# Stored sums in two parts, output weights' pieces at rest for one group, and five half tiles of x in an attention-mix kernel

## The chip, the cores and the metric

The kernel runs on one core of one Trainium2 chip. The metric is the time of one execution on the device in microseconds, as the median of several runs. One execution of the kernel before was also recorded by the hardware profiler; all rows shown here come from that record. The engines are named as the profile names them: PE (TensorE, matmul), PEld (its weight load), DVE (VectorE), ACT (ScalarE), POOL (GpSimd) and SP (SyncE, which issues most transfers).

## The reference

Two attention blocks on the same input of 2048 rows and 1024 columns, 32 heads of 32, mixed by a gate. All in float32.

```python
def _A_ref(x, wqkv, wo):
    ...
    phi = lambda t: jnp.where(t > 0, t + 1, jnp.exp(t)) + 1e-6
    pq, pk = phi(q), phi(k)
    kv = jnp.einsum("bhsd,bhse->bhde", pk, v)
    z = jnp.einsum("bhsd->bhd", pk)
    num = jnp.einsum("bhqd,bhde->bhqe", pq, kv)
    den = jnp.einsum("bhqd,bhd->bhq", pq, z)[..., None] + 1e-6
    o = num / den
    return (lambda x, *d: x.transpose(*d))(o, 0, 2, 1, 3).reshape(B, S, D) @ wo

def _B_ref(x, wqkv, wo):
    ...
    scores = jnp.einsum("bhqd,bhkd->bhqk", q, k) * (Dh ** -0.5)
    p = _softmax(scores, axis=-1)
    o = jnp.einsum("bhqk,bhkd->bhqd", p, v)
    return (lambda x, *d: x.transpose(*d))(o, 0, 2, 1, 3).reshape(B, S, D) @ wo

x = A_x
g = _sigmoid((x * gate_w).sum(-1, keepdims=True))
a = _A_ref(x, A_wqkv, A_wo)
b = _B_ref(x, B_wqkv, B_wo)
return g * a + (1 - g) * b
```

## The kernel before

**Numbers in two parts.** A float32 operand is split into a high part, rounded to the matmul's format by a cast on ScalarE, and a low part, the difference, by a subtraction (`split`, lines 293 to 295: L294 is the cast, L295 the subtraction). A product is three matmuls, high by high, high by low and low by high (`three`, L153, L156, L158), each 128 x 128 by 128 x 512. Results collect in eight PSUM banks.

**Stages, in order of time.**

1. The first v pass (0 to some 50 us): values of block B for the first half of the rows (J = 0), one 128-row piece k of the weights at a time (`load_block`, `split_wv`, `split_x`, `v_pass`). Eight small matmuls on a tile of ones (L627) stand ahead of the first product.
2. The first set of groups, J = 0. Queries and keys of block B are computed for all heads with Strassen's scheme in Winograd's form: seven products instead of eight, on sums and differences of the inputs and the weights. A group (`quad`) makes seven products of twelve matmuls, each into its own bank, combines them on VectorE, and stores four sums. There are eight groups, numbered 0 to 7 here; `quads` runs 0 to 6 of them, and the eighth runs with `change()` beside it.
3. The second v pass (J = 1), begun near 205 us, and the second set of eight groups, near 257 to 410 us, the eighth with `leave()` beside it.
4. The last v pass, from about 410 us to some 523 us: the other 512 columns of v, over all sixteen 128-row units (the stream `linear`, kind "v"). From its middle on the heads' row maxima (`maxima`, L1240 and L1245) and the gate (`gate_step`) run beside it.
5. The heads (some 525 to 2660 us): 32 heads of block B, with scores, exponentials (L1385), sums on POOL (L1467), products with v (L1532), beside the rest of `linear`: block A's keys and values, queries and output.
6. The output of block B (`output`), with Strassen products again, to the end.

**Who orders the work.** Every engine runs its own instructions in the order in which the program writes them. In stages 1 to 3 that order is written out by hand. From stage 4 on a planner writes it: it keeps reckoned clocks for the engines (`T`), costs for each step, and times at which data are reckoned to be there (`xp_ready`, `w_ready`, `q_ready`), and takes the stream that can go on soonest.

**A group and its side work.** `next(side, None)` inside `quad` is one step of side work, seven in a group. The side streams that `quads` runs together are the next group's weights (`quad_weights`, lines 420 to 443, six steps), the late sums of x, transfers, and the pieces of block B's output weights (`parts`). A step of the first, second and third kind writes, for instance, `tensor_sub(w21, w11, w21)` (L432) and then a split. In `change()` and `leave()` the steps are splits.

A group combines and stores like this: the copy of product 0 (L467), the addition of product 1 (L469) and the first store; the additions L476, L477, L478 and the second store; L482, L483 and the third store; L486 and the fourth store. A store (`store`) casts the sum's high part on ScalarE, subtracts on VectorE and issues two transfers of 256 KB to DRAM on SP.

**The pieces of the output weights** (`wo_parts`). 28 pieces are made on POOL: a cast (L513), a subtraction (L514), two transfers (L516), and after three pieces of every seven one more subtraction (L524, L531, L537), with loads of raw weights on POOL's queue (L502). A piece is let go by a tiny copy on ScalarE (L511) that POOL's own tiny copy (L512) waits for. `PIECE_STEP` spaces them: `wait()` lets a turn pass per step until 3.4 turns are over, and each wait uses one turn without giving a step away. Of the 28 pieces, numbers 0 to 18 go out in the first set, one in group 0 and three in each of groups 1 to 6; numbers 19 to 27 go out in the second set: three in group 0, two in group 1, three in group 2, the last at the first step of group 3.

**x in half tiles.** In `linear` each unit of 128 rows needs x in four row pieces of 2 halves: half m = 2n + 0 or 1, with a high and a low part, each 256 KB. Before there are three half tiles, used in turn (`xh_t`): two are the halves of `big[4]`, the third is `xh`. Units 0 to 3 of the last v pass read x from tiles that are still there; the first three halves are asked for at unit 1, and when half m has been used, half m + 3 is asked for. The v weights' store, the heads' v loads (`load_v`), the gate's x loads and the raw weights of the next stage go through the same queue on SP.

**The rows.** For each head the row maxima are turned by a matmul, split (`mh`, `ml`) and written by four transfers into the last rows of the query tiles: `q_first` holds the first 512 columns, `q_rest` the others (`rows`, lines 1247 to 1270).

**The output.** Its first six products (X11 and T1 of three pairs of row tiles) run beside the heads; their banks are copied out on ScalarE (L1695). After the heads come the splits of the next operands (`prep`), the loads of block A's result (`load_ra`) and the other products; results are added on VectorE (L1704 and following).

## Time and profile before

| what | value |
|---|---|
| median of 3 runs | 2822.71 us (2821.43 to 2822.95) |
| the profiled execution: its own time | 2824.52 us |
| its span in the profile | 2822.7 us |
| TensorE's granted clock, mean | 0.998 |
| chain that ended last | TensorE 90%, DMA 2%, "issue" 1% |
| HBM read, written | 314.31 MB, 127.66 MB |
| matmuls | 15880 |

A row of a timeline gives the start in us, the duration in us, the engine, the line of the program, the operation, output and inputs by the program's names, their shapes, and in brackets how long the engine was idle ahead of it and what ended that. SPq and POOL rows of kind DMA are the issuing alone. A row of waits gives the waiting instruction, whom it waited for, the total in us, how often, and the longest. A row of stretches gives the stretch and its length, then busy time and number of instructions of PE, PEld, DVE, ACT and POOL, the granted clock of TensorE as a share of full speed, the mean busy share of the 16 DMA engines, and GB/s. Matmuls are pipelined and their ends are modelled, so that a matmul of 512 columns shows 0.39 us where the next one starts 0.23 us later.

### The profile page before, as it was taken

To read this page: it belongs to the slowest core of one execution; us is meant where nothing else is said; L and a number is where in the kernel's file an instruction comes from. 1 tells how busy PE (TensorE), PEld (TensorE's weight loads), DVE (VectorE), ACT (ScalarE), POOL (GpSimd) and SP (SyncE) were. 2 spreads that over 40 slices of the span, in tenths; PEclk is the share of its full clock that TensorE was granted. 3 is DMA by queue.
4 is the path that set the end of the run, shared out by engine and by line. 5 is a ranking of instruction groups with operands and counts; after the bars stand their busy time and mean duration, and the time that the engine had idled before them with its cause. 6 is when DMAs were issued, how large, how long until landed. Compare 5 with 4: busy or idle time off the path is not lost.

```text
span 2822.7 us, 47003 instructions
## 1 busy us (share of the span) xinstructions
PE 2801.9 (99%) x15880; PEld 2043.3 (72%) x15880; DVE 2330.5 (83%) x3745; ACT 1638.2 (58%) x3095; POOL 2104.1 (75%) x1150
## 2 busy tenths in 40 slices
PE   9999999999999999999999999999999999999999
PEld 8877887777767776677766777776676667666687
DVE  7887865888878888888888888888877888886688
ACT  5334332566666666666766666676666666666522
POOL 0651433699999999999899988989889988888000
PEclk9999999999999999999999999999999999999999
DMA  8997979533343434333433444456575555544774
GB/s 279 301 335 224 293 224 282 175 100 102 103 127 97 106 98 131 94 98 102 126 105 96 106 131 129 151 167 186 172 213 159 145 158 146 145 121 140 255 238 152
DMA packets 403340, 459.52 MB, mean 163 GB/s; under 512 B 106894, under 2 KB 234894, under 8 KB 401308
## 3 DMA queue, kind: packets, MB, share of 16 engines
q1 hardware_dynamic: 381084, 419.03, 47.5%
q0 software_dynamic: 22016, 37.50, 6.2%
q8 instruction: 126, 2.06, 0.3%
q14 instruction: 114, 0.93, 0.1%
HBM read 314.31 MB, written 127.66 MB: 157 GB/s over the span
## 4 chain that ended last, share of the span: by engine, by line
PE 90%; DMA 2%; issue 1%; DVE 0%; ACT 0%; SPq 0%; ACTq 0%; DVEq 0%
PE bank L1382 17%; PE bank L1240 16%; PE bank L1532 16%; PE bank L153 13%; PE bank L156 13%; PE bank L158 13%; PE bank L1304 1%; PE bank L1026 1%; PE bank L915 0%; DMA big<-ra 0%; DMA xh<-xs 0%; SPq L170 0%; PE bank L1296 0%; DMA qk<-mid 0%; DVE big L295 0%
## 5 line engine op out<-in xcount | busy, mean ns | idle before, releaser
L1467 POOL TENSOR_TENSOR big<-big,big 128x512 f32<-128x512 f32 (+2 forms) x694 | 1641.7, 2369 | 107.5 <-ACT big L1385 64.4
L1245 DVE TENSOR_REDUCE mx<-bank 128x1 f32<-128x512 f32 x2048 | 1313.5, 682 | 305.9 <-PE bank L1240 301.9
L1385 ACT ACTIVATE big<-bank 128x512 f32<-128x512 f32 x2048 | 1179.6, 602 | 433.7 <-PE bank L1382 368.4
L1382 PE MATMUL bank<-big,big 128*128 128x512 f32 x1888 | 742.4, 394 | 2.2 <-DMA big<-ml 2.2
L1240 PE MATMUL bank<-big,big 128*128 128x512 f32 x1888 | 739.8, 392 | 1.1 <-ACT big L1385 1.1
L153 PE MATMUL bank<-big,big 128*128 128x512 f32 x1576 | 618.1, 392 | 9.2 <-DVE mid L486 3.9
L158 PE MATMUL bank<-big,big 128*128 128x512 f32 x1572 | 614.9, 391 | 0.5 <-DMA big<-xs 0.2
L156 PE MATMUL bank<-big,big 128*128 128x512 f32 x1576 | 615.4, 390 | 0.0
L1532 PE MATMUL bank<-big,mid 128*32 128x512 f32 x4096 | 454.2, 593 | 0.0
L1382 PEld LDWEIGHTS bank<-big,big 128*128 128x128 f32 x1888 | 354.5, 188 | 127.3 <-issue 48.1
L1240 PEld LDWEIGHTS bank<-big,big 128*128 128x128 f32 x1888 | 355.0, 188 | 75.0 <-ACT big L1385 2.4
L153 PEld LDWEIGHTS bank<-big,big 128*128 128x128 f32 x1576 | 296.9, 188 | 77.6 <-ACT big L294 4.5
L158 PEld LDWEIGHTS bank<-big,big 128*128 128x128 f32 x1572 | 295.8, 188 | 65.9 <-DVE big L295 3.0
L156 PEld LDWEIGHTS bank<-big,big 128*128 128x128 f32 x1576 | 296.7, 188 | 61.3 <-DVE big L295 0.2
L1532 PEld LDWEIGHTS bank<-big,mid 128*32 128x32 f32 x4096 | 143.9, 110 | 264.1 <-issue 263.8
L1483 DVE TENSOR_TENSOR bank<-bank,big 128x512 f32<-128x512 f32 x364 | 251.5, 691 | 5.3 <-ACT big L1385 2.9
L295 DVE TENSOR_TENSOR big<-mid,big 128x512 fp32r<-128x512 f32 (+1 forms) x157 | 122.2, 795 | 44.6 <-ACT big L294 44.2
L294 ACT CAST big<-mid 128x512 fp32r<-128x512 f32 (+1 forms) x157 | 92.8, 618 | 113.1 <-DVE mid L1651 66.0
L1463 POOL TENSOR_TENSOR big<-big,big 128x1536 f32<-128x1536 f32 (+1 forms) x31 | 122.9, 3964 | 44.8 <-ACT big L1385 44.8
L153 PE MATMUL bank<-big,xh 128*128 128x512 f32 x376 | 147.1, 391 | 2.4 <-DMA xh<-xs 2.4
L158 PE MATMUL bank<-big,xh 128*128 128x512 f32 x376 | 146.9, 391 | 0.0
L156 PE MATMUL bank<-big,xh 128*128 128x512 f32 x376 | 146.8, 390 | 0.0
(163 smaller groups left out, 2123.0 us busy)
## 6 DMA issues: line engine op xcount, KB each, us to landing
big<-xs SPq DMA_DIRECT2D x288, 256.0 KB
big<-qk SPq DMA_DIRECT2D x690, 64.0 KB
xh<-xs SPq DMA_DIRECT2D x144, 256.0 KB
qk<-mid SPq DMA_DIRECT2D x128, 256.0 KB
big<-oA SPq DMA_DIRECT2D x84, 256.0 KB
xs<-big SPq DMA_DIRECT2D x64, 256.0 KB
oA<-mid SPq DMA_DIRECT2D x64, 256.0 KB
big<-big POOLq DMA_DIRECT2D x50, 256.0 KB, 5.4
```

The costliest lines, as they stand in the source:

```text
L153: yield nc.tensor.matmul(ps, sh, mh_, start=(kt == 0), stop=False)
L156: yield nc.tensor.matmul(ps, sh, ml_, start=False, stop=(late and last))
L158: yield nc.tensor.matmul(ps, sl, mh_, start=False, stop=last)
L295: eng.tensor_sub(lo, src, f32(hi))
L1240: nc.tensor.matmul(bank[b], q[:, t % TPC * P:(t % TPC + 1) * P], k[:, j * C:(j + 1) * C], start=True, stop=True)
L1245: nc.vector.tensor_reduce(m[:, t, j:j + 1], bank[b], AX.X, ALU.max)
L1382: nc.tensor.matmul(bank[b], k[:, t * P:(t + 1) * P], q_cols(h, j), start=True, stop=True)
L1385: nc.scalar.activation(pr_t[i][:, j * C:(j + 1) * C], bank[b], AF.Exp, scale=SCALE)
L1463: nc.gpsimd.tensor_add(lacc[:, :qp], pr(0)[:, :qp], pr(1)[:, :qp])
L1467: nc.gpsimd.tensor_add(lacc[:, sl], lacc[:, sl], pr(t)[:, sl])
L1483: nc.vector.tensor_add(lacc[:, qp:] if t == NT - 1 else l_b[:, :n], l_b[:, :n], src)
L1532: nc.tensor.matmul(av_b[j * DH:(j + 1) * DH, :], v[:, t, :], pr(t)[:, j * C:(j + 1) * C], start=(t == 0), stop=(t == NT - 1))
```

## The change

Six edits:

- `store` casts the sum's high part, then takes a step of side work, then subtracts and issues its two transfers. The four steps that followed the stores in `quad` go away, so that a group still has seven steps.
- `PIECE_REST = 2`: in the first set the stream `parts` is cut off after 42 steps, six groups instead of seven; it goes on in the second set. By the count of steps, pieces 0 to 15 then go out in the first set, and 16 to 27 in the second: three in group 0, three in group 1, two in group 2, three in group 3, the last in group 4. No piece falls away.
- The last v pass reads x from five half tiles, the two new ones being the halves of `big[5]`. Five halves are asked for at unit 1. `load_past(m)` asks for half m + 5; the three tiles of old serve again from half 32 on, and it is placed ahead of the storing of mixed weights and of `load_v`.
- In `load_block` the v weights of the first piece are loaded ahead of the first 128 columns of x.
- In `rows` the four transfers go in the order high and low for the first columns, then high and low for the others.
- In `output` the copy of the last T1 product out of its bank waits until the first two of the three following `prep` steps are written.

The assignments of 0 to `xp_ready` for the halves 0 to 2, which fall away, name halves that are never loaded.

```diff
@@ -1,6 +1,6 @@
 from collections import deque
 from contextlib import ExitStack
-from itertools import count
+from itertools import count, islice
 
 import concourse.bass as bass
 import concourse.tile as tile
@@ -39,7 +39,7 @@
 WARM = 8
 NE = 3
 AHEAD_X = 3
-PIECE_STEP = 3.4
+PIECE_STEP, PIECE_REST = 3.4, 2
 GATE_STEP, GATE_FROM = 2.3, 20.0
 LATE = 1.0
 MANUAL = {ET.PE, ET.DVE, ET.Activation, ET.SP, ET.Pool}
@@ -133,7 +133,7 @@
 
     k_stack = [big[1], big[3]]
     q_first, q_rest = [big[0][:, :C], big[2][:, :C], None], [big[0], big[2]]
-    xh_t = [big[4][:, :D], big[4][:, D:], None]
+    xh_t = [big[4][:, :D], big[4][:, D:], None, big[5][:, :D], big[5][:, D:]]
     w_t = big[16:20]
     PR, SPARE, LACC = (6, 7, 8, 9, 10, 11, 15, 5, 14), 12, (13, 20)
 
@@ -459,7 +459,9 @@
             return ps
 
         def store(i, jj, src, hi):
-            split(f32r(hi), f32r(src), src, nc.vector)
+            nc.scalar.copy(f32r(hi), src)
+            next(side, None)
+            nc.vector.tensor_sub(f32r(src), src, hi)
             j = 2 * J + jj
             for p, part in enumerate((hi, src)):
                 dma(qk_d[sec][p][g + i][:, j * C:(j + 1) * C], part)
@@ -468,7 +470,6 @@
         next(side, None)
         nc.vector.tensor_add(C11, product(1), P1)
         store(0, 0, C11, H11)
-        next(side, None)
         p3 = product(2)
         next(side, None)
         p5 = product(3)
@@ -477,15 +478,12 @@
         nc.vector.tensor_add(W2, p5, U2)
         nc.vector.tensor_add(P1, p3, W2)
         store(0, 1, P1, H12)
-        next(side, None)
         p7 = product(5)
         nc.vector.tensor_add(W2, p7, W2)
         nc.vector.tensor_add(U2, p7, U2)
         store(1, 1, W2, H22)
-        next(side, None)
         nc.vector.tensor_add(U2, product(6), U2)
         store(1, 0, U2, H21)
-        next(side, None)
 
     def wo_piece(m, i):
         half, l = int(m[1]) - 1, int(m[2]) - 1
@@ -612,9 +610,9 @@
         split(ring_w(k, 0), ring_w(k, 1), raw, nc.vector)
 
     def load_block(k):
+        load_wv(raw_w0[k % 4], k)
         if k == 0:
             load_x(raw_x0[0], 0, 0, 0, 0, P)
-        load_wv(raw_w0[k % 4], k)
         for jj in range(2):
             load_x(raw_x0[k // 2], 0, jj, k, P if k == jj == 0 else 0)
 
@@ -728,7 +726,7 @@
         split_x(raw_x1[1], 1, 1, 3)
         yield
 
-    quads(0, lambda: load_pair(raw_x1[0], 1, 0), reload_wv(), spill_rest(0), parts)
+    quads(0, lambda: load_pair(raw_x1[0], 1, 0), reload_wv(), spill_rest(0), islice(parts, (QUADS - PIECE_REST) * NP))
     load_pair(raw_x1[1], 1, 1)
     quad(0, QUADS - 1, change())
     for k in range(NK):
@@ -872,10 +870,21 @@
     def xstat_lin(n, k, p):
 
         o = (p * HK + k % HK) * P
-        return xh_t[(2 * n + k // HK) % 3][:, o:o + P]
+        return half_at(2 * n + k // HK)[:, o:o + P]
 
     def token(i, t):
         return (t + NT // 2) % NT if chunks[i][0] == "v" else t
+
+    def half_at(m):
+        return xh_t[m % (5 if m < 2 * NT else 3)]
+
+    def load_past(m):
+        if m + 5 < 2 * NT:
+            load_half(m + 5)
+        elif m + 5 == 2 * NT:
+            load_half(2 * NT)
+        elif m >= 2 * NT - 2:
+            load_half(m + 3)
 
     def load_half(m):
 
@@ -886,7 +895,7 @@
         ks = slice(m % 2 * HK, (m % 2 + 1) * HK)
         for p, src in enumerate(oA_d if chunks[i][0] == "o" else xs):
             o = p * HK * P
-            dma(f32(xh_t[m % 3][:, o:o + HK * P].rearrange("p (k c) -> p k c", c=P)), src[t][:, ks])
+            dma(f32(half_at(m)[:, o:o + HK * P].rearrange("p (k c) -> p k c", c=P)), src[t][:, ks])
         xp_ready[m] = T["sp"] + 3.2
 
     def phi(ps, e, n):
@@ -1070,15 +1079,15 @@
                     lin_pe(1.0)
                     if m < 2:
                         yield always
+                if k % HK == HK - 1 and 2 * n + k // HK >= 2 * TPC:
+                    load_past(2 * n + k // HK)
                 store_mix()
                 if kind == "v":
                     if n in (4, 5) and k == 0:
                         load_v(n - 4)
                 if n == 1 and k == 0:
-                    for m in range(2 * TPC, 2 * TPC + 3):
+                    for m in range(2 * TPC, 2 * TPC + 5):
                         load_half(m)
-                if k % HK == HK - 1 and 2 * n + k // HK >= 2 * TPC:
-                    load_half(2 * n + k // HK + 3)
                 if k == 0 and n + 3 == len(units):
                     load_e(0)
                     load_e(1)
@@ -1261,9 +1270,9 @@
             def low(end):
                 rows_ready[h] = end + 2.5
                 nc.vector.tensor_sub(ml, pm[:NT, :P], f32(mh))
-                for i, part in enumerate((mh, ml)):
-                    r = 3 * DH + i
-                    for q, ts in ((q_first[h % 3], slice(0, TPC)), (q_rest[h % 2][:, C:], slice(TPC, NT))):
+                for q, ts in ((q_first[h % 3], slice(0, TPC)), (q_rest[h % 2][:, C:], slice(TPC, NT))):
+                    for i, part in enumerate((mh, ml)):
+                        r = 3 * DH + i
                         dma(f32(q[r:r + 1, :]).rearrange("o (t c) -> o t c", c=P), f32(part[ts]))
 
             give(b, 0.0, [defer(low, end, 0.2, 0)])
@@ -1747,7 +1756,8 @@
                     if i:
                         yield always
                     product(name, n, b, i, i + 1)
-                after(name, n, b)
+                if (name, n) != ("T1", NE - 1):
+                    after(name, n, b)
                 if n + 2 < NE:
                     prep(name, n + 2)
             if n + 2 < NE:
@@ -1782,6 +1792,8 @@
                     load_l(n + 2)
 
         for i in range(AHEAD_X):
+            if i == 2:
+                after("T1", NE - 1, b)
             prepare(i)
         load_l(1)
         load_ra(1)
@@ -1799,8 +1811,6 @@
     assert next(parts, None) is None
     xh_t[2] = sb.tile([P, 2 * HK * P], F32R, name="xh")
     T["sp"] = 0.0
-    for m in range(3):
-        xp_ready[m] = 0.0
     for h in range(2):
         q_ready[h][:] = k_ready[h][:] = [0.0] * NJ
```

## The prediction

> **What bounds the kernel now.** I read the page's engine part, then what TensorE waited for over the whole span, then stretches of it.
>
> ```profile
> span 2822.7 us, 47003 instructions
> PE 2801.9 (99%) x15880; PEld 2043.3 (72%) x15880; DVE 2330.5 (83%) x3745; ACT 1638.2 (58%) x3095; POOL 2104.1 (75%) x1150
> ```
>
> ```profile
> PE bank L153 <- DVE mid L486: 3.9, 1, 3.9
> ...
> PE bank L153 <- ACT big L294: 2.3, 3, 1.2
> PE bank L1382 <- DMA big<-ml: 2.2, 2, 1.6
> PE bank L153 <- DVE mid L483: 1.5, 1, 1.5
> ```
>
> TensorE is never short of work for long, and the change takes no matmul away. So it can win only TensorE's idle time, 2822.7 - 2801.9 = 20.8 us over the span, and the time in which TensorE ran at a lower granted clock:
>
> ```profile
> 205.00:215.00 10.00, 5.18 (x21) 3.31 (x19) 9.00 (x11) 3.32 (x6) 5.26 (x6) 0.98 1.02 383
> 215.00:222.00 7.00, 6.05 (x15) 4.79 (x16) 6.17 (x11) 2.38 (x4) 0.00 (x0) 0.54 0.59 211
> 442.00:454.00 12.00, 9.98 (x40) 6.94 (x40) 6.21 (x9) 3.86 (x6) 4.04 (x4) 1.00 0.92 270
> 525.00:532.00 7.00, 5.88 (x23) 4.49 (x22) 5.38 (x12) 4.05 (x8) 0.52 (x1) 0.76 0.45 154
> ```
>
> The seventh figure is the granted clock. At 0.54 over 7 us some 3.2 us are lost, at 0.76 some 1.7. The largest hole lies at 205 to 222 us, between the first set of groups and the v pass behind it. Whether TensorE or VectorE sets the pace in that set is told by VectorE's waits from 60 to 216 us:
>
> ```profile
> DVE mid L295 <- ACT mid L294: 16.8, 23, 0.7
> ...
> DVE mid L476 <- DMA qk<-mid: 0.5, 1, 0.5
> ```
>
> No row has VectorE waiting for a matmul: there VectorE is behind, and TensorE feels it through weights that come late (L294) and banks that come free late (L483, L486). The 16.8 us are the waits that the change of the store aims at.
>
> **The stored sums.** A store of the second set, with nothing on POOL, shows the pattern; ScalarE's rows, then VectorE's:
>
> ```profile
> 368.62 0.62 ACT L294 CAST mid<-mid 128x512 fp32r<-128x512 f32 x1 [3.53 <-DVE mid L478]
> 369.14 0.62 ACT L294 CAST big<-extra 128x512 fp32r<-128x512 f32 x1
> ```
> ```profile
> 367.85 0.69 DVE L478 TENSOR_TENSOR mid<-bank,mid 128x512 f32<-128x512 f32 x1
> 369.27 0.69 DVE L295 TENSOR_TENSOR mid<-mid,mid 128x512 fp32r<-128x512 f32 x1 [0.73 <-ACT mid L294]
> 369.88 0.68 DVE L295 TENSOR_TENSOR big<-extra,big 128x512 fp32r<-128x512 f32 x1
> ```
>
> In this second store of its group (after L478) VectorE waits 0.73 us for the cast, subtracts at 369.27 and splits the side step's weights at 369.88, free at 370.48. In the new order the side step's subtraction comes first, but its own cast stands second on ScalarE and ends at 369.76: VectorE waits until 369.80, then does two subtractions of 0.60 (the pitch of these rows) and is free at 371.0, 0.53 later. The third store is alike: 0.53. In the first one the side step begins with L432, which needs no cast: that hides 0.6, the wait for the second cast eats it, gain 0.06. In the fourth the step has no VectorE work. So a group costs VectorE 0.53 + 0.53 - 0.06 = 1.0 us **more**, where the wait of 0.73 seems to promise a gain. Behind the longer waits stand the additions that free TensorE's banks and the next group's weights. In the last group, whose side steps are splits only, the first store loses as well: 1.64. SP gets the side step's transfers ahead of the store's two; nobody waits for these but L476 (0.5 above).
>
> Part of the added wait is free, since POOL and VectorE keep each other out:
>
> ```profile
> 139.34 0.61 POOL L513 CAST big<-zrep 128x512 fp32r<-128x512 f32 x1 [3.17 <-DMA woS<-big]
> 140.04 1.29 POOL L514 TENSOR_TENSOR big<-zrep,big 128x512 fp32r<-128x512 f32 x1
> ...
> 142.41 1.30 POOL L531 TENSOR_TENSOR zrep<-zrep 128x512 f32<-128x512 f32 x1
> ```
> ```profile
> 141.81 2.46 DVE L432 TENSOR_TENSOR mid<-mid,mid 128x512 f32<-128x512 f32 x1
> ```
>
> L432 took 2.46 us instead of 0.68 and ended just behind POOL's L531. A piece of the output weights holds POOL 0.61 + 1.29 and, in 3 of 7, another 1.30: 2.46 us on average. The first set's first six groups run 16 pieces in 121.9 us (L469 of groups 0 and 6 below), so POOL is in these 32% of the time, and I take 0.7 us per group of the 1.0. Ends: 0, if TensorE's lead hides it; 1.0.
>
> **The rest of the pieces.** Counting the steps (each piece waits 2.4 steps of 7 per group), pieces 16 to 18 leave group 6 of the first set, and the second set has pieces through group 3 instead of group 2. What they cost VectorE:
>
> ```profile
> 58.10 0.68 DVE L469 TENSOR_TENSOR mid<-bank,mid 128x512 f32<-128x512 f32 x1
> ...
> 180.02 0.68 DVE L469 TENSOR_TENSOR mid<-bank,mid 128x512 f32<-128x512 f32 x1
> ...
> 285.89 0.68 DVE L469 TENSOR_TENSOR mid<-bank,mid 128x512 f32<-128x512 f32 x1
> ...
> 327.14 0.68 DVE L469 TENSOR_TENSOR mid<-bank,mid 128x512 f32<-128x512 f32 x1
> ...
> 343.82 0.68 DVE L469 TENSOR_TENSOR mid<-bank,mid 128x512 f32<-128x512 f32 x1
> ```
>
> The quiet group takes 343.82 - 327.14 = 16.7 us; two groups with five pieces took 41.25, so a piece costs 1.6; in the first set (121.9 - 6 x 16.7) / 16 = 1.4. I take 1.5. The three that go:
>
> ```profile
> 192.66 1.18 DVE L295 TENSOR_TENSOR mid<-mid,mid 128x512 fp32r<-128x512 f32 x1
> 193.77 2.45 DVE L295 TENSOR_TENSOR big<-mid,big 128x512 fp32r<-128x512 f32 x1
> ...
> 202.14 2.37 DVE L295 TENSOR_TENSOR big<-xh,big 128x512 fp32r<-128x512 f32 x2
> ...
> 211.16 1.18 DVE L295 TENSOR_TENSOR mid<-mid,mid 128x512 fp32r<-128x512 f32 x1
> 212.27 3.03 DVE L295 TENSOR_TENSOR big<-mid,big 128x512 fp32r<-128x512 f32 x2
> ```
>
> Against 0.69 for one and 0.69 + 0.60 for two that is 0.49 + 1.76 + 1.08 + 0.49 + 1.74 = 5.6 us, all in groups 6 and 7.
>
> **First set, sum.** VectorE's last addition L486 moves by 6 x 0.7 = +4.2, + 1.0 and 1.64 in the last two groups, - 5.6: +1.2. TensorE waits for it at the v pass's last bank, so it goes on 1.2 later; but some 4 us of waiting move ahead, into the groups (late weights), and the hole there shrinks from 1.5 + 3.9 = 5.4 to about 2.6. How the clock answers to 2.6 no row tells: the 3.9 were followed by 0.54, the 1.1 at 525 us by 0.76 for half as long; I take half, -1.6. Net -0.4. Ends: -5.4 - 3.2 = -8.6 (added waits hidden); +5.8 (added waits whole, 8.6, and only half of the 5.6 gone).
> The Trainium skill, TensorE: Matmul & The Clock Gate, "The HAM clock gate", has the clock fall after an idle window of about 3.4 us. This trace differs: it fell behind a wait of 1.1 us. By the page a hole of 2.6 would leave the clock whole.
>
> **Second set.** TensorE does not wait here now. The step after L478 gives the weights of the next group's third product: ready 1.91 us after its start (367.85 to 369.76).
>
> ```profile
> 334.21 0.69 DVE L478 TENSOR_TENSOR mid<-bank,mid 128x512 f32<-128x512 f32 x1
> ```
> ```profile
> 339.00 0.39 PE L153 MATMUL bank<-big,big 128*128 128x512 f32 x1
> ```
>
> 339.00 (that product's first matmul, by count) - 336.12 = 2.9 us to spare in group 3. After the change VectorE is 3 x 0.7 later and has two more pieces ahead of that step, 3.0: 5.1 - 2.9 = **+2.2**. In group 4 the same reckoning leaves nothing over, and the quiet groups then win it back. Ends 0.1 and 4.6 (1.0 per group, 1.9 per piece).
>
> **Five half tiles.** The longest wait in the v pass, and SP's queue:
>
> ```profile
> 443.68 0.47 PE L153 MATMUL bank<-big,big 128*128 128x512 f32 x1 [1.02 <-DMA big<-xs]
> ```
> ```profile
> 437.60 0.86 SPq L170 DMA_DIRECT2D big<-xs  x2
> ...
> 440.11 5.65 SPq L170 DMA_DIRECT2D big<-xs  x2
> ```
>
> The half needed at 442.7 was issued at 437.60, three halves ahead. Four more transfers at the start of the pass and two halves (5.5 us) more lead put each half ahead of its matmuls even with SP's block of some 5 us: -2.0, the idle time of 442 to 454 (ends 0 and -2.3). On SP they pass the mixed weights' stores and the heads' v loads; the first ten stand ahead of the unit's own store and beside POOL's q and k transfers, none of which any row above waits for. At the pass's end two pairs fewer are issued, just where L1385 waits at 525 us behind a cast that waits for its load:
>
> ```profile
> 525.62 0.62 ACT L844 CAST big<-extra 128x512 fp32r<-128x512 f32 x1 [1.28 <-DMA extra<-in_a_wqkv]
> ```
>
> 1.1 of wait and 1.7 of clock hang on it; that load is issued when `extra` comes free, so lighter traffic shortens only its landing: I take -1.2 of the 2.8 (ends 0, -2.8).
>
> **Smaller edits.** The rows' low half for the first columns becomes the second transfer of four instead of the third, one issue (0.7) sooner; of the waits of 2.2 that is up to 1.3, but SP's reckoned times shift and the planner orders all that follows anew: -0.7 (ends +1, -1.3). The deferred copy at the end:
>
> ```profile
> 2681.35 0.50 PE L153 MATMUL bank<-big,big 128*128 128x512 f32 x1 [1.19 <-ACT big L294]
> ```
> ```profile
> 2697.75 1.14 ACT L294 CAST big<-mid 128x512 fp32r<-128x512 f32 x2 [5.71 <-issue]
> ```
> ```profile
> 2688.06 0.75 DVE L1704 SCALAR_TENSOR_TENSOR big<-mid,omg_sb,big 128x512 f32<-128x512 f32 x1 [2.12 <-DMA big<-ra]
> ```
>
> The cast no longer stands behind the copy, and TensorE starts 1.2 earlier (its bank stays held meanwhile, one of eight); but the chain of waits runs from the ra transfer through VectorE to the cast at 2697.75, untouched, and there TensorE gives it back: 0 (ends 0, -1.2). First load: the warming matmuls run until the first real one, 0.
>
> **Sum.** -0.4 + 2.2 - 2.0 - 1.2 - 0.7 = -2.1. The profiled run took 2824.5 us, 1.8 more than its span; the median of the runs is 2822.7, 1.8 below that run. On the median: **2820.6**.
>
> **Rivals.** (A) The forecast; own range 2816 to 2824; 0.38. (B) The added waits cost TensorE nothing, because its lead and POOL's share hide them: -8.6 + 0.1 - 2.0 - 1.2 - 0.7 = -12.4, 2810.3. For it: in 60 to 180 us TensorE waited little; against: VectorE never waits for TensorE there. 0.28. (C) Slower: VectorE's added waits count whole in both sets, and POOL's backlog keeps half of the stretches: +5.8 + 4.6 - 2.0 and nothing else = +8.4, 2831.1; it decides once both sets together lose over 7.6. Against: POOL's 32%. 0.10. (D) The half tiles do nothing, because SP's 5 us block moves ahead of the new loads: 2820.6 + 2.0 + 1.2 = 2823.8; 0.14. (E) The clock stays full after the smaller hole: -1.6, 2819.0; against: the 0.76 behind 1.1 us. 0.10. This one is what the Trainium skill's page, TensorE: Matmul & The Clock Gate, would have.
>
> A measurement of this kernel tells about 0.2% (5.6 us) from no change. Faster than 2817.1: all of B, 0.07 of A, 0.04 of E: 0.39. Slower than 2828.3: C and 0.01 of D: 0.11. Same 0.50. Range 2808 to 2827.
>
> **What would show it.** A store's subtraction behind the side step's, with waits near 1.3 us before the second store's side subtraction; L469 intervals of some 21 us with pieces, 17.7 without; L486 near 217; a TensorE wait on L294 near 340; no xs waits in the v pass; a TensorE wait near 2698. If L486 lies before 211 with no low clock behind it, the working of the added waits is wrong.

## The result, and the profile after

The changed kernel took 2836.93 us, the median of 5 runs (2832.86 to 2838.91); the kernel before, run beside it, took 2822.95 (2821.43 to 2827.13). The ratio is 1.0044, with an interval of 1.003 to 1.0059: **slower**, by 0.44%, a small loss that is clear of the noise. The forecast was 2820.6, in a range of 2808 to 2827. The first part of the page of the changed kernel:

```profile
span 2835.1 us, 46999 instructions
PE 2806.8 (99%) x15880; PEld 2046.2 (72%) x15880; DVE 2332.9 (82%) x3745; ACT 1638.7 (58%) x3095; POOL 2109.2 (74%) x1150
```

The same number of matmuls keeps TensorE busy 4.9 us longer (2806.8 against 2801.9), and its idle time went from 20.8 to 28.3 us. Lower clock accounts for the first: by the clock records of the two traces TensorE ran at half clock for 20.5 us where it was 10.2, half of the difference being 5.1 us. What TensorE waited for in the changed kernel (the instruction, whom it waited for, total us, times, longest):

```profile
PE bank L153 <- ACT big L294: 8.3, 6, 3.0
PE bank L583 <- POOL mid L575: 3.7, 1, 3.7
PE bank L153 <- DVE mid L485: 2.2, 1, 2.2
...
PE bank L153 <- DVE mid L483: 2.0, 1, 2.0
PE bank L1249 <- ACT mid L358: 1.7, 1, 1.7
```

Some lines have moved: the first addition of a group is now L471, the last L485, the cast of a stored sum L462 and its subtraction L464. Waiting for the cast of weights (L294) rose from 2.3 to 8.3 us; the waits for x (big<-xs and xh<-xs) in the last v pass fell from 1.9 to 1.1 us in sum; a wait for POOL's L575, the gate, is new, and so is one for ScalarE's copy L358. The stretches in which these waits lie, changed kernel, columns as before:

```profile
216.00:228.00 12.00, 7.80 (x22) 5.58 (x20) 10.52 (x17) 4.04 (x7) 0.00 (x0) 0.72 0.52 183
128.00:139.00 11.00, 8.04 (x29) 5.95 (x28) 9.03 (x11) 2.37 (x5) 7.65 (x12) 0.84 1.04 316
325.00:334.00 9.00, 6.73 (x21) 4.74 (x20) 7.03 (x9) 2.37 (x5) 5.65 (x8) 0.81 0.81 284
466.00:484.00 18.00, 12.51 (x45) 9.80 (x44) 6.50 (x10) 5.86 (x10) 7.68 (x6) 0.81 0.89 309
```

Before, the low clock stood in two places (215 and 525 us). Now it stands in four, each beside a wait of 2 to 4 us.

Where the 12.4 us of span were lost, by the start of each stage (TensorE's matmuls counted in the trace; us from the start of the span):

| stretch | before | after | difference | forecast |
|---|---|---|---|---|
| up to the second set of groups | 257.4 | 263.2 | +5.8 | -0.4 |
| second set | 152.3 | 157.4 | +5.1 | +2.2 |
| last v pass, up to the first product with v | 140.8 | 146.2 | +5.4 | -3.2 |
| from there to the end | 2272.2 | 2268.3 | -3.9 | -0.7 |

All three stages ahead of the heads went the wrong way. VectorE's first addition of groups 0, 6 (first set), 4 and 5 (second set) of the changed kernel:

```profile
59.03 0.69 DVE L471 TENSOR_TENSOR mid<-bank,mid 128x512 f32<-128x512 f32 x1
...
188.74 0.68 DVE L471 TENSOR_TENSOR mid<-bank,mid 128x512 f32<-128x512 f32 x1
...
359.48 0.68 DVE L471 TENSOR_TENSOR mid<-bank,mid 128x512 f32<-128x512 f32 x1
...
377.14 0.69 DVE L471 TENSOR_TENSOR mid<-bank,mid 128x512 f32<-128x512 f32 x1
```

The six groups of the first set with pieces took 129.7 us against 121.9, 1.3 more per group; the quiet group of the second set 17.66 against 16.68. What VectorE waited for in those six groups, before and then after:

```profile
DVE mid L295 <- ACT mid L294: 13.1, 18, 0.7
DVE big L295 <- ACT big L294: 1.1, 3, 0.4
```

```profile
DVE big L295 <- ACT big L294: 15.7, 19, 1.3
DVE mid L464 <- ACT mid L462: 4.4, 6, 0.7
```

14.2 us became 20.1. That is 5.9 over six groups, or 0.98 per group: the reordering that was to use a wait made more of it. One store in the quiet group (the second, after L479) shows how, first ScalarE, then VectorE:

```profile
367.25 0.62 ACT L462 CAST mid<-mid 128x512 fp32r<-128x512 f32 x1 [3.28 <-DVE mid L479]
367.78 0.61 ACT L294 CAST big<-mid 128x512 fp32r<-128x512 f32 x1
```

```profile
366.48 0.69 DVE L479 TENSOR_TENSOR mid<-bank,mid 128x512 f32<-128x512 f32 x1
368.42 0.69 DVE L295 TENSOR_TENSOR big<-mid,big 128x512 fp32r<-128x512 f32 x1 [1.25 <-ACT big L294]
369.03 0.69 DVE L464 TENSOR_TENSOR mid<-mid,mid 128x512 fp32r<-128x512 f32 x1
```

The sum's cast was ready at 367.87, but the subtraction that needs it (L464) stands behind one that needs the second cast, ready at 368.39. VectorE stands idle for 1.25 us where it stood for 0.73.

### The profile page after: what moved, and what is told of

The parts are those of the page before. It is cut to its first block, busy times and chain, and to the rows that moved or that the text cites. A ratio compares the mean times of both kernels' runs of the same rounds, so it can differ in the third digit from the quotient of the medians.

```text
span 2835.1 us, 46999 instructions
## 1 busy us (share of the span) xinstructions
PE 2806.8 (99%) x15880; PEld 2046.2 (72%) x15880; DVE 2332.9 (82%) x3745; ACT 1638.7 (58%) x3095; POOL 2109.2 (74%) x1150
## 4 chain that ended last, share of the span: by engine, by line
PE 86%; DMA 1%; issue 1%; DVE 0%; ACT 0%; SPq 0%; POOL 0%; DVEq 0%; ACTq 0%; POOLq 0%
PE bank L1391 17%; PE bank L1249 16%; PE bank L1541 16%; PE bank L153 12%; PE bank L158 12%; PE bank L156 12%; PE bank L1313 1%; PE bank L1035 1%; DMA big<-ra 0%; PE bank L924 0%; PE bank L1305 0%; DMA zrep<-in_xT 0%; DMA big<-xs 0%; DMA extra<-in_a_wqkv 0%; PE bank L995 0%
## 5 line engine op out<-in xcount | busy, mean ns | idle before, releaser
L295 DVE TENSOR_TENSOR big<-mid,big 128x512 fp32r<-128x512 f32 (+1 forms) x157 | 116.3, 757 | 73.6 <-ACT big L294 73.3
L294 ACT CAST big<-mid 128x512 fp32r<-128x512 f32 (+1 forms) x157 | 92.6, 617 | 106.0 <-DVE mid L1660 64.5
L462 ACT CAST mid<-mid 128x512 fp32r<-128x512 f32 x64 | 39.7, 621 | 188.0 <-issue 128.1
L1549 ACT COPY mid<-bank 128x512 f32<-128x512 f32 x32 | 18.8, 587 | 213.1 <-PE bank L1541 206.1
L153 PE MATMUL bank<-big,xh 128*128 128x512 f32 x360 | 140.9, 391 | 0.0
```

Source lines behind the costliest of these rows:

```text
L153: yield nc.tensor.matmul(ps, sh, mh_, start=(kt == 0), stop=False)
L295: eng.tensor_sub(lo, src, f32(hi))
```

## The experiments

**Names.** A kernel called b_ is the kernel before with one part of the change added; a_ is the changed kernel with one part undone or altered; w_ is built to beat both. The table gives VectorE's time for the first six groups of the first set, the start of stages on TensorE, and the span, all of the one profiled execution; then the median of the runs and its ratio, with the interval, to the kernel before run beside it (medians of 2822.95 to 2824.25).

| kernel | six groups | second v pass | second set | last v pass | first product with v | span | median | ratio |
|---|---|---|---|---|---|---|---|---|
| before | 121.9 | 204.7 | 257.4 | 409.7 | 550.6 | 2822.7 | 2822.95 | 1 |
| after | 129.7 | 211.7 | 263.2 | 420.6 | 566.8 | 2835.1 | 2836.93 | 1.0044 (1.003 to 1.0059) |
| a_old_store | 125.8 | 208.5 | 257.6 | 411.3 | 552.3 | 2820.4 | 2822.53 | 0.9998 (0.9987 to 1.0009) |
| b_store | 131.8 | 214.3 | 270.6 | 423.0 | 563.6 | 2834.6 | 2833.97 | 1.0039 (1.0024 to 1.0055) |
| b_rest | 121.2 | 203.9 | 253.8 | 406.5 | 545.6 | 2815.6 | 2819.97 | 0.9987 (0.9978 to 0.9997) |
| b_five | 128.6 | 212.2 | 261.2 | 413.5 | 552.8 | 2822.5 | 2823.81 | 0.9996 (0.9986 to 1.0007) |
| b_small | 121.5 | 205.4 | 257.2 | 409.8 | 549.6 | 2820.8 | 2823.86 | 1.0003 (0.9992 to 1.0013) |
| a_three | 131.4 | 213.0 | 264.5 | 422.0 | 564.6 | 2834.3 | 2834.95 | 1.0044 (1.0029 to 1.0059) |
| b_five_stag | 124.3 | 206.2 | 260.5 | 412.8 | 549.3 | 2817.9 | 2819.85 | 0.9985 (0.9976 to 0.9994) |
| a_early | 117.0 | 216.3 | 259.8 | 412.1 | 552.2 | 2821.0 | 2819.62 | 0.9985 (0.9976 to 0.9994) |
| a_early_three | 114.0 | 212.3 | 255.8 | 408.1 | 546.8 | 2815.8 | 2818.87 | 0.9985 (0.9975 to 0.9994) |
| b_store_early | 113.4 | 201.3 | 251.9 | 406.9 | 545.4 | 2816.1 | 2820.33 | 0.9989 (0.9979 to 0.9998) |
| w_early_three | 114.3 | 201.5 | 254.5 | 406.8 | 546.5 | 2816.4 | 2817.59 | 0.9976 (0.9967 to 0.9985) |
| w_early_stag | 114.7 | 201.9 | 254.0 | 406.3 | 542.2 | 2810.6 | 2811.95 | 0.9955 (0.994 to 0.997) |

**How far one execution can be trusted.** Up to the second set, before, b_five and b_five_stag run the same instructions. Yet their six groups took 121.9, 128.6 and 124.3 us, and their second v pass began at 204.7, 212.2 and 206.2. A difference of a few us in that stage between two profiles tells nothing by itself; those below are of groups of kernels, and the times of many runs stand beside them.

### Which part of the change costs

**a_old_store**: the changed kernel with the sums stored in one piece again.

```diff
-            nc.scalar.copy(f32r(hi), src)
-            next(side, None)
-            nc.vector.tensor_sub(f32r(src), src, hi)
+            split(f32r(hi), f32r(src), src, nc.vector)
...
+        next(side, None)
         p3 = product(2)
```

> The kernel after with the store in one piece again, the side step behind it. Theory 'added waits' (VectorE's longer waits for the second cast are what made the groups 10.8 us slower): the three moved pieces now help alone, VectorE's last addition of the first set ends before 211 us, no half clock behind it, and the last v pass begins at 400 to 406 us instead of 420.6. The time is then some 2820 if the last v pass keeps its loss of 7 us, some 2813 if that loss only followed from the late groups. Rival 'moved pieces' (the second set cannot carry three more pieces, and that is what costs): the last v pass still begins after 415 us and the time stays above 2831.

**b_store**: the kernel before with the split store alone, the opposite edit.

> The kernel before with the split store alone, all pieces where they were. Theory 'added waits': 1.0 us more per group on VectorE, whole, in the first set: the second v pass begins at 210 us or later (204.7 before) with a hole as long as before behind it, and the last v pass begins at 416 to 421 us; time 2830 to 2836. Rival 'moved pieces': the groups end within 2 us of the kernel before, time 2821 to 2825.

Undoing the split store takes the whole loss away (0.9998); the split store alone brings nearly all of it (1.0039). Of the kernels that store in one piece the six groups took 121.9, 125.8, 121.2, 128.6, 121.5 and 124.3, a mean of 123.9; of those with the split store 129.7, 131.8 and 131.4, a mean of 131.0: **7.1 us more, 1.2 per group**, and the lowest of the one kind lies above the highest of the other. In a_old_store the last v pass begins at 411.3, between what the theory (400 to 406) and the rival (after 415) had said: the old store takes the loss away, but the gain of the moved pieces does not show there. In b_store it begins 2 us later than its theory had it. b_store's VectorE in its six groups, then TensorE's longest wait from 50 to 420 us:

```profile
DVE big L295 <- ACT big L294: 16.0, 20, 1.3
DVE mid L464 <- ACT mid L462: 4.4, 6, 0.7
```

```profile
PE bank L153 <- DVE mid L479: 6.1, 1, 6.1
```

The waits for casts are those of the changed kernel within 0.3 us. VectorE's lag ends in one wait of 6.1 us of TensorE for a bank, in the v pass behind the set.

**b_rest**: the kernel before with the moved pieces alone.

```diff
-PIECE_STEP = 3.4
+PIECE_STEP, PIECE_REST = 3.4, 2
...
-    quads(0, lambda: load_pair(raw_x1[0], 1, 0), reload_wv(), spill_rest(0), parts)
+    quads(0, lambda: load_pair(raw_x1[0], 1, 0), reload_wv(), spill_rest(0), islice(parts, (QUADS - PIECE_REST) * NP))
```

> The kernel before with the three pieces moved alone. Theory 'moved pieces win in the first set what they lose in the second': VectorE's blocked time in the last two groups of the first set goes (5.6 us), one more group of the second set takes 19 to 20 us instead of 16.7 without TensorE waiting over 2 us; time 2815 to 2821. Rival 'they buy nothing': 2822 to 2826.

The moved pieces alone gain 0.13% (0.22 to 0.03), some 3.7 us; the last v pass begins 3.2 us sooner, and the second set takes as long as before (152.7 and 152.3 us). That holds with the old store. With the split store too (after, a_three) the second set takes 157.4 and 157.5, with the split store alone (b_store) 152.3. So the 5.1 us of the second set belong to **both edits together**: with either alone TensorE has no wait in the second set that the trace shows.

**b_small**: the kernel before with the order of the first load, the order of the rows' transfers and the deferred copy, as in the diff of the change, and nothing else.

> The kernel before with the three small edits alone: first load, rows' transfers, deferred copy of T1. Theory: 2820 to 2824 on a kernel before of 2823, with the wait of 1.19 for L294's cast at 2681 gone and a wait of 1 to 2 us in the 20 us behind it. Rival (the rows' order or the deferred copy costs): 2826 or more.

No change in time (1.0003). The wait of 1.19 at 2681 us is gone, and TensorE waits a little later instead:

```profile
2687.36 0.50 PE L158 MATMUL bank<-big,big 128*128 128x512 f32 x1 [1.79 <-DVE big L295]
```

So the start that is won is given back within some 9 us, for a subtraction (L295) that the deferred copy does not touch. In the changed kernel that wait is 1.92 us, at 2702.70.

### Why the split store costs

**a_early**: the changed kernel with the side steps' casts written a step earlier than the subtractions that use them (that of `part(5, w21)` two steps earlier), in the weights' steps and in `change()`. ScalarE then has the side step's cast done before the stored sum's cast comes.

```diff
+        def cast(s, raw):
+            nc.scalar.copy(ring_w(quad_ring(J, f, s), 0), raw)
+
+        def low(s, raw):
+            n = quad_ring(J, f, s)
+            nc.vector.tensor_sub(ring_w(n, 1), raw, f32(ring_w(n, 0)))
...
+        cast(1, w12)
         yield
         nc.vector.tensor_sub(w21, w11, w21)
-        part(1, w12)
+        low(1, w12)
...
         part(4, w11)
+        cast(2, w12)
+        cast(5, w21)
         yield
-        part(2, w12)
+        low(2, w12)
         yield
-        part(5, w21)
+        low(5, w21)
```

> The kernel after, with the side steps' casts of the first, second and third store (and of the splits beside the last group of the first set) written one step earlier, so that they stand ahead of the store's cast on ScalarE; the same instructions, no other change. Theory 'second cast' (what the split store costs is the wait for the side step's own cast, 17.7 us for a group without pieces against 16.7): such a group now takes 15.2 to 15.4 us, the groups with pieces some 2.4 us less each than after, the last v pass begins at 400 to 405 us instead of 420.6, and the time is 2808 to 2816. Rival 'POOL and DMA' (the groups are late because of blocked subtractions and landings, whatever the order): a group without pieces stays above 17 us, the last v pass still begins after 415 us, and the time stays above 2830.

**a_early_three**: the same with three half tiles of x.

> The same with three half tiles of x. Theory 'the half tiles trade one wait for another' (no gain and no loss from them): time within 3 us of the kernel with the early casts and five halves, 2808 to 2816; waits for xs of 2 to 5 us in the last v pass in place of the wait for the gate's sum. Rival 'they help once the groups are in time': 3 us or more slower than with five.

In both kernels one early cast in `change()` (the second one) writes a tile that the second product of the last group still reads: that product takes a replaced high part of one piece of x, and the first sum that the last group stores differs for it. These two kernels serve for their times alone. The six groups fall to 117.0 and 114.0 us, below every kernel without the early casts, and a quiet group of a_early to 15.2. But most of that is lost in the last group, where TensorE waits for that cast (a_early; 8.8 us in a_early_three):

```profile
197.06 0.79 PE L153 MATMUL bank<-big,big 128*128 128x512 f32 x1 [12.08 <-ACT big L730]
```

```profile
195.39 0.59 ACT L479 COPY mid<-bank 128x512 f32<-128x512 f32 x1 [7.21 <-DMA qk<-mid]
```

The cast stands on ScalarE behind a copy that waits 7.21 us for a store to land. So a_early's last v pass begins at 412.1 and its time is 2819.62, where the theory had 400 to 405 and 2808 to 2816, and the rival over 415 and over 2830: the mechanism is confirmed in the groups, the time is not what it promised. The edit to `change()` is a poor one, and the kernels that follow leave it out.

**b_store_early**: b_store with the early casts of the weights alone (the diff above).

> The kernel before with the split store alone, and the casts of the next group's weights (in the side steps of the groups only) issued one step earlier than the subtractions that use them. Theory (VectorE stands behind the side step's cast, which comes second on ScalarE): a quiet group of the second set takes 15.2 us instead of 17.7, the first six groups of the first set together 114 to 119 us (mean of the split store 131.0, of the old one 124.4), the last v pass begins at 402 to 410 (423.0 with the split store alone), time 2812 to 2820. Rival (the order of the casts is not what costs; the store's late transfers or POOL do): the six groups stay above 126 us, the time above 2828.

The same store, at the same place, with nothing but the casts' order altered: 2820.33 us instead of 2833.97, and the last v pass begins at 406.9 instead of 423.0. VectorE's waits in the six groups of b_store_early, then the first addition of groups 0 and 6 and of a quiet group of the second set and the next:

```profile
DVE mid L474 <- ACT mid L472: 4.4, 6, 0.7
DVE big L429 <- ACT big L425: 2.1, 4, 0.8
DVE big L295 <- ACT big L294: 1.1, 1, 1.1
```

```profile
58.18 0.68 DVE L481 TENSOR_TENSOR mid<-bank,mid 128x512 f32<-128x512 f32 x1
...
171.56 0.68 DVE L481 TENSOR_TENSOR mid<-bank,mid 128x512 f32<-128x512 f32 x1
...
340.41 0.68 DVE L481 TENSOR_TENSOR mid<-bank,mid 128x512 f32<-128x512 f32 x1
...
355.78 0.68 DVE L481 TENSOR_TENSOR mid<-bank,mid 128x512 f32<-128x512 f32 x1
```

7.6 us of waits instead of 20.4; 113.4 us for the six groups instead of 131.8, 15.4 for the quiet one. (Three pieces fewer fall into the six groups, 13 instead of 16 by count of POOL's rows; at the prediction's 1.5 us for a piece, that would be some 4.5 of the 18.4.) This is the wait that the split store was to use, now really used. The second store of that quiet group shows it, by VectorE's two subtractions behind the addition L489:

```profile
346.66 0.69 DVE L489 TENSOR_TENSOR mid<-bank,mid 128x512 f32<-128x512 f32 x1
347.27 0.68 DVE L429 TENSOR_TENSOR big<-mid,big 128x512 fp32r<-128x512 f32 x1
348.08 0.69 DVE L474 TENSOR_TENSOR mid<-mid,mid 128x512 fp32r<-128x512 f32 x1
```

The side step's subtraction follows the addition at once, and the sum's begins 0.13 us behind the end of that. Against the rival (the late transfers or POOL cost, not the casts' order): the edit does not touch them, and the loss is gone. The time missed its expectation (2812 to 2820) by 0.3 us.

### The half tiles

**b_five**: the kernel before with five half tiles alone, as in the diff of the change.

> The kernel before with the five half tiles alone. Theory 'crowded start': the groups end at 409.7 us as before, but units 8 to 12 take 34 us or more, with late gate loads and a copy on ScalarE that waits for a v store; time 2826 to 2829. Rival 'late groups' (the half tiles by themselves do what the prediction said): units 4 to 8 lose their waits for xs, units 8 to 12 stay near 31.3 us, time 2818 to 2821.

**a_three**: the changed kernel with three half tiles, the opposite edit.

> The kernel after with three half tiles of x again. Theory 'crowded start' (the two more halves asked for at unit 1 put 1 MB more ahead of the v stores and the gate's loads): units 8 to 12 of the last v pass take 31 to 33 us as before (38.2 after), no wait of TensorE for POOL's gate sum, some waits for xs instead (2 us); time 2830 to 2833. Rival 'late groups' (the groups' lateness alone crowds that stage): units 8 to 12 still take over 36 us, the wait for the gate sum stays, and the time is 2836 to 2840.

**b_five_stag**: five half tiles, the two extra ones asked for one unit and two units later.

```diff
-                    for m in range(2 * TPC, 2 * TPC + 5):
+                    for m in range(2 * TPC, 2 * TPC + 3):
                         load_half(m)
+                if n in (2, 3) and k == 0:
+                    load_half(2 * TPC + 1 + n)
```

> The kernel before with five half tiles, but of the two added halves one is asked for at unit 2 and one at unit 3, not all five at unit 1. Theory 'crowded start' (the MB asked for at once pushes the v stores and the gate's loads back, TensorE then waits 2 us for the gate's sum and its clock falls): no wait for POOL's gate sum above 1 us, no half clock there, time 2818 to 2821. Rival 'the DMA engines are full in that stage whatever the order': waits of 2 us or more in sum stay in the last v pass, time 2822 to 2826.

Asked for all at once the halves give nothing (0.9996); staggered, 0.15% (0.24 to 0.06), some 4 us. The profiles show what is won and what is lost, by units of the last v pass:

| kernels | units 4 to 8 | units 8 to 12 | TensorE's wait for the gate's sum |
|---|---|---|---|
| before | 29.0 | 31.3 | 0 |
| the seven others with three halves | 27.5 to 32.2 | 31.3 | 0 |
| five at once: b_five | 25.9 | 35.3 | 2.17 |
| five at once: after, a_old_store, a_early | 25.9 to 29.3 | 35.6 to 38.3 | 2.44 to 3.75 |
| five staggered: b_five_stag, w_early_stag | 25.6 | 32.6 and 33.0 | 1.04 and 1.44 |

So in b_five both sides were right in part, and its 2823.81 lies between the two ranges: the halves win 3.1 us in units 4 to 8 and lose 4.0 behind them. In a_three the wait for the gate is gone and units 8 to 12 are back at 31.3, as its theory had it; its time lies between the two ranges. b_five_stag's wait of 1.44 is above the 1 us that its theory allowed, its time is within.

What goes wrong at once is best seen in the changed kernel, in SP's queue, ScalarE and TensorE:

```profile
431.50 3.96 SPq L170 DMA_DIRECT2D big<-xs  x8
435.70 2.68 SPq L170 DMA_DIRECT2D xh<-xs  x2
...
440.57 2.96 SPq L170 DMA_DIRECT2D v<-mid  x2
```

```profile
449.51 1.23 ACT L358 COPY mid<-bank 128x512 f32<-128x512 f32 x2 [11.80 <-DMA v<-mid]
```

```profile
468.99 0.50 PE L1249 MATMUL bank<-big,big 128*128 128x512 f32 x1 [1.75 <-ACT mid L358]
...
476.92 1.87 PE L583 MATMUL bank<-ones,mid 128*128 128x1 f32 x8 [3.75 <-POOL mid L575]
```

Ten transfers of 256 KB are issued between two stores of v. The next copy out of a bank (L358) needs the tile that the store reads, and ScalarE stands still for 11.80 us until the store has landed. The next store of v needs that copy, and the gate's next loads of x stand behind this store on SP: the second load of the gate is issued 30.6 us after the start of the pass, where it was 23.6 in the kernel before. ScalarE's gate steps then wait for their loads, the gate's last addition on POOL ends 6.9 us later in the pass than before, and the sum on TensorE (L583) comes 3.75 us late and is followed by low clock. In b_five the same wait of ScalarE is 7.76 us, the load is issued at 26.5, and the last addition ends 1.9 us later, while TensorE comes 3.0 us earlier by what it won in units 4 to 8: only the two together make its wait of 2.17 (either alone leaves at most 0.3), and 1.7 us of low clock come on top. In b_five_stag ScalarE waits for no store, the load is issued at 23.6, and TensorE waits 1.44 at full clock. Before, the copy that waited longest for a store of v:

```profile
442.74 0.59 ACT L358 COPY mid<-bank 128x512 f32<-128x512 f32 x1 [3.28 <-DMA v<-mid]
```

The ten transfers are not all of that wait: with three halves and the split store it is 6.40 (b_store) and 8.59 us (a_three), without a wait for the gate's sum. With three half tiles the waits for x are longer again (in a_three 3.99 us at one matmul), and the median is 2834.95 instead of 2836.93, within what the runs can tell. The pass as a whole takes 146.2 us in the changed kernel, 141.0 with five halves and the old store (a_old_store), 142.6 and 140.6 with three halves and the split store (a_three, b_store), 140.8 before: the loss of 5.4 shows only where both edits are in.

### A version that beats both

**w_early_three**: the changed kernel with the weights' early casts and three half tiles. **w_early_stag**: the same with five staggered ones.

> The changed kernel with the weights' casts in the side steps of the groups one step earlier, the last groups' side steps as the change has them, and three half tiles of x. Theory: quiet group 15.2 us, six groups 114 to 119, no wait of TensorE for L730's cast near 190 to 203, last v pass from 398 to 406, time 2808 to 2817. Rival (the gain is given back at the next stage, behind the transfers of the last group, where ScalarE's copy waits for a store that stands behind the weights' loads): a wait of TensorE of 5 us or more between 185 and 220 stays, time 2818 or more.

> The same with five half tiles, the two extra ones asked for at units 2 and 3. Theory (five halves are worth nothing or little in the time, because the gate's sum takes the place of the waits for x): within 3 us of the kernel with three, a wait of TensorE for the gate's POOL row of 1 to 4 us in place of some 5 us of waits for x. Rival (the halves do gain their 2 us once the wait for the gate is short): 2 to 4 us faster than with three.

w_early_stag takes 2811.95 us: 0.45% (0.6 to 0.3) faster than the kernel before. For w_early_three the time (2817.59) lies 0.6 beyond what the theory gave and just short of the rival's; the hole of 5 us that the rival named is there, as three waits of 2.0 to 2.2, 6.2 in sum. For w_early_stag the halves bring 5.6 us, more than either side had expected (the two intervals still touch: 0.994 to 0.997 and 0.9967 to 0.9985). The stretches of units 4 to 8 and 8 to 12 of the last v pass show 3.2 us won and 1.3 given back, of 3.8 that the whole pass takes less (135.9 against 139.7); first w_early_three, then w_early_stag:

```profile
428.54:457.38 28.84, 26.70 (x114) 20.82 (x113) 11.29 (x17) 7.83 (x12) 9.75 (x9) 1.00 0.92 277
457.38:488.70 31.32, 31.32 (x147) 26.19 (x146) 23.23 (x35) 10.41 (x18) 12.96 (x10) 1.00 0.87 282
```

```profile
428.06:453.67 25.61, 25.61 (x114) 21.21 (x113) 11.28 (x17) 7.20 (x11) 8.09 (x8) 1.00 0.99 296
453.67:486.28 32.61, 31.57 (x147) 26.11 (x146) 23.23 (x35) 11.35 (x19) 14.72 (x12) 1.00 0.94 312
```

What sets the pace of the first set in w_early_stag is told by its six groups:

```profile
59.20:173.90 114.70, 114.70 (x508) 94.98 (x507) 103.51 (x138) 44.66 (x92) 66.70 (x86) 1.00 0.96 301
```

TensorE is busy for all of the 114.70 us at full clock, 19.1 per group: it has become the bound there. In the kernel before VectorE needed 20.3 per group, so TensorE fell behind by 1.2 each. What is late next stands in the last two groups:

```profile
193.49 0.59 ACT L479 COPY mid<-bank 128x512 f32<-128x512 f32 x1 [5.79 <-DMA qk<-mid]
```

```profile
203.97 0.69 DVE L487 TENSOR_TENSOR mid<-bank,mid 128x512 f32<-128x512 f32 x1 [4.29 <-DMA qk<-mid]
```

ScalarE and VectorE wait for stores of sums to land; in a_early the store in question was issued behind six loads of the weights of v. Moving those loads was not tried.

## Why the prediction was wrong, by its own steps

Between the forecast of -2.1 us and the 12.4 that the span gained lie 14.5 us. Three steps failed: the discount on VectorE's added waits, the clock that was to recover behind the first set, and the half tiles that were to cost nothing on SP's queue.

- **The pattern of the store: right.** 1.0 us more per group was worked out from the row of the wait and the order of the casts; the quiet group took 0.98 more, the waits rose by 0.98 per group in the first set, and a store's second subtraction ends some 0.5 later, as drawn.
- **"Part of the added wait is free, since POOL and VectorE keep each other out … I take 0.7": this step failed.** VectorE's waits for casts in the six groups are 13.8 to 14.5 us in all six profiles with the old store and 19.7 to 20.5 in all three with the split one: 6.0 more, the whole 1.0 per group. The rest of the six groups' time, which the step would have 6 x 0.3 = 1.8 us shorter, is 109.8 in the mean of the six and 110.9 in that of the three. Its spread (106.9 to 114.7 with the old store) is too wide to say more than that no gain shows. In sum 6 x 0.7 = 4.2 was 7.1 to 7.8. That POOL is busy in a third of the time did not show as a discount; why not is not shown. A likely reason is that moving a wait of VectorE does not move POOL's pieces away from VectorE's rows.
- **The last two groups: right.** 1.0 + 1.64 - 5.6 = -3.0 was the forecast; they took 32.1 us instead of 35.2, -3.1. That it fits to 0.1 is partly luck, since b_five took 32.4 with no piece moved. The pieces' own term is borne out with the split store: 38.0 in b_store against 32.1 in after and a_three, 6.0 where 5.6 was reckoned.
- **"The hole there shrinks … to about 2.6" and half of the clock comes back: wrong as a consequence.** The last addition came at 220.8 (217 forecast), the two waits there are 2.0 and 2.2, and the waits that moved ahead into the groups are large enough to lower the clock there too (0.84 at 128 to 139 us). Instead of -0.4 the stage cost 5.8. Low clock was forecast to shrink, and it grew: this step, too, failed. The Trainium skill's section on the HAM clock gate (TensorE: Matmul & The Clock Gate), by which a hole of 2.6 would leave the clock whole, is not borne out: behind single waits of 2.96 (128 to 139 us) and 2.27 (325 to 334) stand 0.84 and 0.81.
- **Second set, +2.2: right in kind, too small, and a group early.** The wait of TensorE for the weights of a third product came, of 2.27 us:

```profile
328.15 0.50 PE L153 MATMUL bank<-big,big 128*128 128x512 f32 x1 [2.27 <-ACT big L294]
```

  It came in group 2, not in group 3 near 340, and with its low clock the set cost 5.1. The reckoning added the waits and the moved pieces one by one; b_store and b_rest show that each alone costs this stage next to nothing (0.0 and +0.4), and that both together cost 5. Its upper end of 4.6 is also missummed: with 1.0 per group and 1.9 per piece the terms give 3 + 3.8 - 2.9 = 3.9.
- **Five half tiles, -2.0 and -1.2: this step failed too, and by stages it is the largest miss (-3.2 forecast, +5.4 measured).** "... the first ten stand ahead of the unit's own store … none of which any row above waits for" was the error: the row of L358 with 3.28 us of waiting for a store of v was in the trace before and was not looked at. The step also left out the gate, whose loads share the queue and whose sum TensorE meets in units 8 to 12. The waits for x fell by 0.8 us; 5.5 us of other waits (3.75 and 1.75) and a low clock came. Alone, the halves are worth nothing (0.9996). The -2.0 was not too large as a size (3.1 to 3.4 in units 4 to 8 of b_five and b_five_stag); what was wrong is that nothing behind them would give it back. Of the -1.2, no part came through shorter landing: the wait at the pass's end is 1.15 us (544.57) where it was 1.12, and only its low clock is absent.
- **Small edits: -0.7 was not to be seen** (1.0003 for the three alone). The copy at the end was given back, as worked out, but earlier than near 2698 and for another instruction. The 3.9 us that the last stretch gained in the profile are not explained by them: b_rest, which does not touch that stretch, shows 2.1 of it.
- **The rivals.** C (both sets lose whole, 2831.1) came nearest, and its price for the sets fits: +5.8 and +5.1 against +5.8 and +4.6. The fit is partly luck: its +5.8 is 6.0 in the six groups and -0.2 in the last two, the measured one comes from +7.8 and -3.1, and its 4.6 should be 3.9. It still credited the half tiles with -2.0, and that stage gave +5.4. Its chance of 0.10 was too low because "POOL's 32%" counted as evidence against it, and because it was required to keep half of the stretches, which turned out to be gone. D (the half tiles do nothing) has the right value for them alone, by b_five, but for another reason than it gave. E fell with the clock, B with the waits.

Still open: why the split store and the moved pieces together cost 5 us in the second set where each alone costs none. In the profiles of after and a_three group 2 ends some 6 us later against the start of the set than before. Of these, 2 are added idle time of VectorE; the rest lies in VectorE's rows; that these ran longer beside POOL's pieces is likely, but was not separated. Why the last v pass loses 5.4 us only with five halves and the split store together is open as well. Whether another spacing of the pieces would remove that was not tried.

## What to carry to other kernels

When work is put between a cast and the subtraction that waits for it, look at what that work itself waits for: if it begins with a cast on the same engine, it stands behind the first one, and the wait grows (0.73 to 1.25 us here) until its own cast is issued a step earlier. A cost that was worked out whole from the order of the instructions should not be discounted by a statistical overlap with a third engine unless a row shows the overlap; and where two engines run near the same pace (20.3 against 19.1 us per group), each us per group counts in full. Deeper prefetch on one queue is paid by what stands behind it: before asking for more at once, read which engine waits for the next store and the next loads on that queue, and spread the requests over units.

## What the runs showed of the hardware that was not expected

- The low clock comes in whole periods. In the clock records of the fourteen traces every stretch of low clock before the end of the execution is at half clock and lasts 3.41 us or a whole multiple of it, and in one execution they all begin whole multiples of 3.41 us apart. So each trace can be cut into such periods, and what decides is how long TensorE stands idle within one of them (the gate's sum, eight matmuls of one column, counted as idle). Of the periods at full clock in all fourteen traces, none of 11441 with less than 1.7 us of idle time was followed by half clock, 5 of 10 with 1.7 to 1.85, and 26 of 26 with more. Two periods of the changed kernel around its wait of 2.96 us, then the two around its wait of 1.92 (at 2702.70):

```profile
131.79:135.20 3.41, 0.46 (x3) 0.07 (x1) 2.09 (x5) 1.14 (x2) 1.87 (x4) 1.00 1.06 305
135.20:138.61 3.41, 3.41 (x8) 2.45 (x9) 2.76 (x5) 1.23 (x3) 1.92 (x5) 0.50 0.91 292
```

```profile
2698.62:2702.03 3.41, 2.16 (x10) 1.47 (x8) 1.49 (x3) 0.00 (x0) 0.00 (x0) 1.00 1.13 326
2702.03:2705.44 3.41, 2.74 (x12) 2.29 (x13) 3.35 (x7) 1.14 (x2) 0.53 (x2) 1.00 1.05 320
```

  A wait that falls across a boundary is split: the 1.92 us are 1.25 and 0.67, and the clock stayed full. The 1.79 of b_small lie in one period, and the clock fell behind them. In the kernel before, the 1.12 us at 525 and part of the gate's one-column matmuls make 1.77 in one period. So for a wait of 1.7 to 3.4 us its position decides over 1.7 us or more of clock, and the boundaries lie differently against the start in each execution (the first of them at 2.98 us before, 2.08 in the changed kernel).
- The same instructions took from 121.9 to 128.6 us in six groups in three executions, about as much as the loss that was to be found there (7.1); the times of whole runs of the kernel before spread far less in proportion (2817.4 to 2830.9 us, 0.5%).
- A store of v was awaited 11.80 us by the engine that wanted its tile again, with ten loads of 256 KB issued ahead of it on the same queue; before, with six, the longest such wait was 3.28, but in a_three, also with six, it was 8.59.
